# Sliding-window attention and a gated FFN on one core: key blocks of 64 on four TensorE tiles, and key blocks of 32 on eight

## The chip, the cores and the metric

The kernel runs on one core of a Trainium2 chip. The metric is the device time of one execution in microseconds, the median over runs. Each execution computes the whole output from inputs that lie in the chip's memory, weights included. TensorE does the matrix multiplications into PSUM (eight banks), ScalarE (ACT) and VectorE (DVE) take them out of it, GpSimd (POOL) and SyncE (SP) mostly issue transfers (DMA).

## The reference

Attention with 8 batches, 8 heads, 576 tokens, head size 64, in which a query sees itself and the 63 keys before it; its output, put together over the heads, goes through a gated feed-forward block.

```python
def _attn_ref(q, k, v):
    B, H, S, D = q.shape                       # 8, 8, 576, 64
    window = 64
    scores = (1.0 / np.sqrt(D)) * np.matmul(q, k.transpose(0, 1, 3, 2))
    rel = np.arange(S)[:, None] - np.arange(S)[None, :]
    scores = np.where((rel >= 0) & (rel < window), scores, -1000000000.0)
    scores = scores - np.max(scores, axis=-1, keepdims=True)
    attn = np.exp(scores)
    attn = attn / (np.sum(attn, axis=-1, keepdims=True) + 1e-09)
    return np.matmul(attn, v)

def _moe_ref(x, w_gate, w_val, w_out):         # x: 4608 x 512, weights 512 x 1536, 1536 x 512
    g = x @ w_gate
    return (g * (1.0 / (1.0 + np.exp(-g))) * (x @ w_val)) @ w_out
```

## The kernel before

The 4608 tokens are nine tiles of 512. Tile t = 0 to 6 is tokens 0 to 511 of batch t, tile 7 (`LAST`) the last 64 tokens of all eight batches, tile 8 tokens 0 to 511 of batch 7. Every operand of TensorE is bf16, sums are fp32 in PSUM. The order of instructions on each engine is written out by hand (`manual_schedule`): an engine runs its instructions in program order, and what one engine needs from another it waits for on semaphores.

One turn of the main loop (L740) is one tile t. First its attention, laced into the output projection of tile t - 1; then its gate and value products with the weights `wg` and `wv` (`gate_value`, L444): twelve blocks of 128 of the 1536 hidden columns, each eight matmuls of 512 columns (L448), a Silu on ACT (L441) and a multiplication on DVE into `hT` (L442). The projection of tile t (`project`, L488, matmuls L457) is four blocks s of 128 tokens, 12 matmuls of 512 columns each; `project_end` copies a block out of PSUM (L464) and stores it (L483).

Attention of a tile t from 1 to 6 and of tile 8, before the change. Queries and keys lie transposed: `queries[t]` and `kT` hold 64 features of an even head on partitions 0 to 63 (h = 0) and of an odd head on 64 to 127 (h = 1), for four pairs of heads u. Two pairs make a half w of the heads.

- `scores(t, w)` (L252): eight blocks j of 64 keys. A block meets the 128 queries from its own first key on, for two head pairs x and two heads h: four matmuls with 64 x 64 weights (L269), which lie in four quarters of the TensorE array. 32 matmuls for a half of the heads, 64 for a tile. ACT takes the exponential (L282) of two times 960 columns, DVE multiplies by a mask of ones and zeros (L285) and adds the two parts that a query's sum consists of into `both` (L290).
- `sums(t, w)` (L321): four matmuls of a matrix of ones with `both` (L302, 512 columns), then ACT takes the logarithm (L316) and the exponential of its negative (L319), which is the inverse of the sum.
- `mix_all(t)` (L416): 64 matmuls of the values with the exponentials (L386), then DVE multiplies by the inverse (`scale`, L402) into `xT`, the input of the gate.

TensorE's order in a tile is: scores of half 0; projection block 0 and five matmuls of block 1; scores of half 1 and sums of half 0; the rest of block 1 and block 2; sums of half 1 and the products; block 3; then the gates. In PSUM, `two[0]` and `two[1]` are two pairs of banks, for scores and products; `out_tile` gives banks 4 and 5 in turn to projection and gate, `d_tile` banks 6 and 7 to sums and values of the gate.

Loads: `load_qk(t + 2)` is issued on POOL's queue in the gates of tile t, q in four transfers (L91), k in sixteen (L126). DVE transposes one head pair at a time (`turn`: q at L207, k at L217) after gate blocks 1, 4, 7 and 10 of tile t - 1 (in tile 1's turn after blocks 6, 7, 9 and 10). v comes in eight transfers (`load_halves`, L152), on SP into a staging tile which POOL casts (L177), or on POOL directly. A run of 16 tokens of q is one row of a transfer, so queries are in the order of their place in a run: `blocks` (L68) picks the queries of some keys out of that order.

In tile 7 a query's two key blocks are not neighbours in one sequence, and `scores` and `mix` use twice as many matmuls, each with 64 queries.

Of the kernel before, what the change touches and what calls it, by code (L numbers as in the profile page):

```python
# [8 lines left out]
P = 128  # L9
# [8 lines left out]
def kernel(  # L18
# [13 lines left out]
    NT = NTOK // 512  # L32
    TURNED = 1
    LAST = NT - 2

    ctx.enter_context(tc.manual_schedule())
    cst = ctx.enter_context(tc.tile_pool(name="cst", bufs=1))
# [17 lines left out]
    vl = v12[:].rearrange("r g i (c w h) d -> r (g i) c w h d", c=2, w=2)  # L55
    vb = [cst.tile([P, 8, 2, 2, D], BF16, name=f"vb{i}") for i in range(2)]
    eb = [cst.tile([P, 17, 64], BF16, name=f"eb{i}") for i in range(4)]
    identb = cst.tile([P, P], BF16, name="identb")
    ones = cst.tile([P, 512], BF16, name="ones")
    tri = cst.tile([P, 2, 64], BF16, name="tri")  # L60
# [4 lines left out]
    def batch(t):  # L65
        return t if t < LAST else t - 1

# [80 lines left out]
    def load_halves(eng, dst, t, hds=range(H)):  # L148

        for hd in hds:  # L150
            w, x, h = hd // 4, hd // 2 % 2, hd % 2
            eng.dma_start(  # L152
                dst[64 * x:64 * x + 64, :, w, h],
                v[batch(t), hd, 0:512].rearrange("(j r) d -> r j d", r=64),
            )

    def load_last_v():
        for c in range(2):
# [11 lines left out]
    def stage_v(t):  # L170
        new_v(t)
        load_halves(nc.sync, staged[t, "v"], t)
# [30 lines left out]
    def turn_q(t, u):  # L203

        if u == 0:
            queries[t] = att.tile([P, 4, 512], BF16, name="qT", tag="qT")
        nc.vector.transpose(  # L207
            queries[t][:, u, :].rearrange("r (e x) -> r e x", e=16),
            staged[t][0][:, u].rearrange("r (e d) -> r e d", d=D)[:, :, 0:32],
        )  # L210
# [38 lines left out]
    def half(x):  # L249
        return slice(64 * x, 64 * x + 64)  # L250
# [57 lines left out]
    def room(n):  # L308
        return fsb.tile([P, 2, 512], FP32, name="r", tag="r", bufs=4)[:, 0:n]

    def turned(ap):

        return ap.rearrange("r (e x) -> r x e", e=16)

    def log(r, d_ps):
        nc.scalar.activation(r, d_ps, AF.Ln)  # L316
# [4 lines left out]
    def sums(t, w):  # L321
        d = d_tile(), d_tile()
        totals(t, w, d)
        for x in range(2):
            r = room(1)[:, 0]
            if t == NT - 1:
                log(r.rearrange("r (x e) -> r x e", e=16), turned(d[x]))
            else:
                log(r, d[x])
            invert(r)  # L330
            inverse[t, 2 * w + x] = r

# [62 lines left out]
    def scale(t, u, o_ps):  # L395
        if u == 0:
            xT[t] = att.tile([P, 4, 512], BF16, name="xT", tag="xT")
        x, r = xT[t][:, u, :], inverse.pop((t, u))
        if t == NT - 1:
            x, o_ps = x.rearrange("r (x e) -> r x e", e=16), turned(o_ps)  # L400
            r = r.rearrange("r (x e) -> r x e", e=16)
        nc.vector.tensor_mul(x, o_ps, r)  # L402

    taken = {"a": 0, "g": 0, "v": 0}
# [1 line left out]
    def take(tag):  # L406
        taken[tag] += 1
        return taken[tag] % 2 ^ 1
# [3 lines left out]

    def d_tile():
        return bank[6 + take("v")]

    def mix_all(t):  # L416
        tiles = wide(), wide()
# [26 lines left out]
    def gate_value(t, m):  # L444
        pair = gate_tiles()
        for ps, w in zip(pair, (wg, wv)):
            for c in range(4):
                nc.tensor.matmul(  # L448
                    ps[:], w[:, c, P * m:P * m + P], xT[t][:, c, :],
                    start=(c == 0), stop=(c == 3),  # L450
                )
        gate_end(t, m, pair)
# [9 lines left out]
    def project_end(t, s, o_ps, copy=nc.vector.tensor_copy):  # L462
        os_ = fsb.tile([P, 512], FP32, name="os_", tag="os_", bufs=4)
        copy(os_[:], o_ps[:])  # L464
        rows = out[S * batch(t):S * batch(t) + 512]
        if t < TURNED or t == NT - 1:
            if t < TURNED:
                rows = rows.rearrange("(r e) f -> e r f", e=4)[s]
            else:
                rows = rows[P * s:P * s + P]  # L470
            if t < TURNED or s == 0:
                for i in range(2):
                    nc.sync.dma_start(rows[half(i)], os_[half(i)])
            else:
                nc.sync.dma_start(rows, os_[:])
            return
# [197 lines left out]
    for m in range(12):  # L674
        if m < 4:
            if m == 2:
                pairs += [gate_tiles(), gate_tiles()]
                for i, w in enumerate((wg, wv)):
                    for n in (2, 3):
                        for c in range(4):  # L680
                            gate_one(0, n, pairs[n][i], w, c)
            gate_end(0, m, pairs[m])
        else:
            gate_value(0, m)
        if m == 3:
            for x in range(2):
                for c in range(2):
                    nc.vector.tensor_copy(
                        mask[half(x), 0, c],
                        tri[half(x), x ^ c].rearrange("r (y e) -> r e y", e=16),  # L690
                    )
            for i in (1, 2, 4):
                nc.vector.tensor_copy(mask[:, i:2 * i], mask[:, 0:i])
            for E in eb:
                nc.vector.memset(E[:, 0], 0.0)
        if m in (7, 10):
# [12 lines left out]
        if m == 9:  # L709
            for u in range(2):  # L710
                turn_q(1, u)
# [26 lines left out]
        project_end(0, s, tiles[s], on_a if s < 2 else on_v)  # L738

    for t in range(1, NT):  # L740
        if t > 1:
            set_exp()
            scores(t, 0)
            project(t - 1, 0)
            if t == 2:
                stage_v(3)
# [24 lines left out]
        turns = (6, 7, 9, 10) if t == 1 else (1, 4, 7, 10)  # L771
        for m in range(12):
            gate_value(t, m)
            if m in turns and t + 1 < NT:
# [35 lines left out]
```

## Time and profile before

| | us |
|---|---|
| runs, median of 3 (lowest, highest) | 324.4 (324.14, 324.52) |
| profiled execution, first to last instruction | 322.4 |
| TensorE busy in it | 317.1 |
| VectorE busy | 219.5 |
| ScalarE busy | 166.8 |
| GpSimd busy | 145.8 |
| attention stage of tile 2, from the last gate of tile 1 to the first of tile 2 (104.73 to 117.91) | 13.18 |

All times in views of the trace are microseconds from the span's start. A timeline line gives start, length, engine, source line, operation, the tile written and those read, the shape and how many instructions were put together; lengths of neighbouring groups overlap, since matmuls are pipelined: a matmul of 512 columns is recorded as 0.38 us long, and they start 0.22 us apart. A line of groups ends with the busy time, the mean length of one in ns, and after the next bar how long the engine had been idle before them and what ended most of that. "two", "one", "eb", "both" are the program's names of tiles; "issue" is time for which the profile shows no releaser.

### The profile page before, as it was taken

Reading aid. Unit: us, or ns where it says so; the run is one execution under the profiler, and the core shown is the slowest. Engines: PE = TensorE matmul, PEld = TensorE weight load, DVE = VectorE, ACT = ScalarE, POOL = GpSimd, SP = SyncE. Lnnn points to the kernel's source line nnn. Section 1 sums busy time; section 2 is a strip of 40 time slices with the busy share of each in tenths; the row PEclk is TensorE's granted clock in tenths of the full one; section 3 lists DMA queues with packets and bytes.
Section 4 is the critical chain, followed back from the end, with each engine's and each line's share of the span. In section 5 each row is a group of like instructions: output and inputs, shape, how many; then the busy total and the mean of one; then the engine's idle time right before and its main releaser. Section 6 shows DMA issues by size and latency. Waiting matters only on the chain.

```text
span 322.4 us, 7047 instructions
## 1 busy us (share of the span) xinstructions
PE 317.1 (98%) x2774; PEld 150.5 (47%) x2774; DVE 219.5 (68%) x349; ACT 166.8 (52%) x239; POOL 145.8 (45%) x259
## 2 busy tenths in 40 slices
PE   7999999999999999999999999999999999999995
PEld 3644444444544444444444544454444544444443
DVE  5866846597676867777688766876696586773432
ACT  5954665356633763368335833665347533773310
POOL 4955656966075795586125989462200000000000
PEclk9999999999999999999999999999999999999999
DMA  7999999999989999949903999799401400020012
GB/s 252 202 197 198 206 142 223 150 158 126 199 162 198 114 166 195 195 74 226 198 11 46 170 163 97 57 211 179 87 3 35 100 2 0 14 86 36 0 28 103
DMA packets 83521, 40.35 MB, mean 125 GB/s; under 512 B 64160, under 2 KB 78752, under 8 KB 83488
## 3 DMA queue, kind: packets, MB, share of 16 engines
q0 software_dynamic: 51488, 22.59, 58.3%
q1 hardware_dynamic: 31456, 16.79, 21.0%
q10 hardware_dynamic: 544, 0.52, 0.5%
q8 instruction: 21, 0.34, 0.4%
q14 instruction: 12, 0.10, 0.1%
HBM read 53.02 MB, written 9.44 MB: 194 GB/s over the span
## 4 chain that ended last, share of the span: by engine, by line
PE 95%; DMA 2%; DVE 1%; SPq 1%; issue 0%; DVEq 0%
PE one L448 56%; PE one L457 29%; PE two L269 3%; PE two L386 2%; DMA k_f<-in_k_dram 2%; PE one L424 2%; PE one L302 1%; PE one L499 1%; SPq L77 1%; PE two L424 1%; DVE kT L198 0%; PE two L702 0%; PE one L351 0%; DVE qT L573 0%; PE two L302 0%
## 5 line engine op out<-in xcount | busy, mean ns | idle before, releaser
L441 ACT ACTIVATE sg<-one 128x512 f32<-128x512 f32 x107 | 63.9, 597 | 113.6 <-PE one L448 86.7
L442 DVE TENSOR_TENSOR hT<-sg,one 128x512 bf16<-128x512 f32 x107 | 74.2, 694 | 61.9 <-PE one L448 57.8
L448 PE MATMUL one<-xT,wg 128*128 128x512 bf16 x416 | 106.8, 379 | 0.0
L448 PE MATMUL one<-xT,wv 128*128 128x512 bf16 x416 | 106.8, 379 | 0.0
L457 PE MATMUL one<-wo,hT 128*128 128x512 bf16 x420 | 95.2, 380 | 0.0
L126 POOL DMA_DIRECT2D k_s<-in_k_dram x112 | 60.8, 552 | 29.0 <-DMA q_s<-in_q_dram 21.8
L448 PEld LDWEIGHTS <-wv 128*128 128x128 bf16 x416 | 40.7, 98 | 49.1
L448 PEld LDWEIGHTS <-wg 128*128 128x128 bf16 x416 | 40.5, 98 | 48.8
L457 PEld LDWEIGHTS <-hT 128*128 128x128 bf16 x420 | 39.0, 98 | 46.7 <-issue 2.0
L282 ACT ACTIVATE eb<-two 128x960 bf16<-128x960 f32 (+1 forms) x32 | 29.5, 975 | 15.1 <-PE two L269 15.0
L217 DVE STREAM_TRANSPOSE kT<-k_s 128x512 bf16<-128x512 bf16 x28 | 36.1, 1289 | 0.0
L285 DVE TENSOR_TENSOR eb<-eb,mask 128x960 bf16<-128x960 bf16 (+1 forms) x32 | 21.1, 658 | 11.5 <-ACT eb L282 11.5
L402 DVE TENSOR_TENSOR xT<-two,r 128x512 bf16<-128x512 f32 x34 | 21.8, 686 | 6.4 <-PE two L386 4.8
L177 POOL CAST vb<-v_f 128x512 bf16<-128x512 f32 x20 | 11.5, 619 | 30.3 <-DMA v_f<-in_v_dram 19.4
L319 ACT ACTIVATE r<-r 128x512 f32<-128x512 f32 (+1 forms) x34 | 22.2, 657 | 1.0
L207 DVE STREAM_TRANSPOSE qT<-q_s 128x512 bf16<-128x512 bf16 x32 | 22.3, 701 | 0.1
L316 ACT ACTIVATE r<-one 128x512 f32<-128x512 f32 x31 | 18.3, 590 | 4.7 <-PE one L302 4.7
L91 POOL DMA_DIRECT2D q_s<-in_q_dram x24 | 13.1, 566 | 4.3 <-DVE qT L207 4.2
L290 DVE TENSOR_TENSOR both<-eb 128x512 bf16<-128x512 bf16 x32 | 13.6, 425 | 1.1
L152 POOL DMA_DIRECT2D vb<-in_v_dram x16 | 11.1, 718 | 4.6 <-DMA wo<-in_moe_w_out_dram 3.4
L507 ACT ACT_TABLE_LOAD x9 | 11.5, 1283 | 2.0 <-issue 1.9
L98 POOL DMA_DIRECT2D q_s<-in_q_dram x16 | 8.6, 627 | 7.5 <-DVE qT L207 7.5
(128 smaller groups left out, 198.4 us busy)
## 6 DMA issues: line engine op xcount, KB each, us to landing
k_s<-in_k_dram POOLq DMA_DIRECT2D x112, 56.0 KB, 4.8
q_s<-in_q_dram POOLq DMA_DIRECT2D x24, 248.0 KB, 5.9
v_f<-in_v_dram SPq DMA_DIRECT2D x40, 128.0 KB
wg<-in_moe_w_gate_dram POOLq DMA_DIRECT2D x5, 256.0 KB, 8.4
wv<-in_moe_w_val_dram POOLq DMA_DIRECT2D x5, 256.0 KB, 9.4
q_f<-in_q_dram SPq DMA_DIRECT2D x4, 256.0 KB
wo<-in_moe_w_out_dram POOLq DMA_DIRECT2D x2, 512.0 KB, 9.9
vb<-in_v_dram POOLq DMA_DIRECT2D x16, 64.0 KB, 4.6
```

Source lines behind the costliest of these rows:

```text
L126: nc.gpsimd.dma_start(k_s[p0:p0 + 32, g, :, 0:w], k[b, a:H:2, s:s + P].rearrange("u (r e) d -> r u (e d)", e=4) [:, :, 32 * c:32 * c + w],)
L207: nc.vector.transpose(queries[t][:, u, :].rearrange("r (e x) -> r e x", e=16), staged[t][0][:, u].rearrange("r (e d) -> r e d", d=D)[:, :, ...
L217: nc.vector.transpose(dst[:, u, :].rearrange("r (g x e) -> r g e x", g=4, e=4), k_s[:, :, u].rearrange("r g (e d) -> r g e d", d=D)[:, :, ...
L282: nc.scalar.activation(flat, s_ps[h][:].rearrange("r a b -> r (a b)")[:, 0:n], AF.Exp, scale=0.125)
L285: nc.vector.tensor_mul(flat, flat, mask[:].rearrange("r j c e y -> r (j c e y)")[:, 0:n])
L316: nc.scalar.activation(r, d_ps, AF.Ln)
L319: nc.scalar.activation(r, r, AF.Exp, scale=-1.0)
L402: nc.vector.tensor_mul(x, o_ps, r)
L441: nc.scalar.activation(sg[:], g_ps[:], AF.Silu)
L442: nc.vector.tensor_mul(hT[t][:, m, :], sg[:], v_ps[:])
L448: nc.tensor.matmul(ps[:], w[:, c, P * m:P * m + P], xT[t][:, c, :], start=(c == 0), stop=(c == 3),)
L457: nc.tensor.matmul(o_ps[:], hT[t][:, c, P * s:P * s + P], wo[:, c, :], start=(c == 0), stop=(c == 11),)
```

## The change

For six tiles (t = 2 to 6 and 8, `NARROW`) the attention is done in another form.

- Keys come in 16 blocks i of 32. A block meets the 96 queries from its first key on (64 and 32 at the end). A matmul has weights of 64 x 32 (`scores_n`) and, for the products and the sums, 32 x 64 (`mix_n`, `totals_n`): four head pairs u times two heads h lie on eight parts of the array. Scores are 128 matmuls, products 128, sums 8 of 512 columns.
- The four head pairs of a tile go together: scores in one visit, sums in one, products in one. The scores fill 960 columns of two bank pairs and 480 of banks 6 and 7; the exponential is taken in two pieces (960 and 480 columns) for each h. The mask multiplies only the first and the last third of each block's 96 queries. `both` is the sum of three parts.
- The logarithm and its exponential are taken over 1024 columns at a time. Products of u = 0 and 1 go to banks 6 and 7, of u = 2 and 3 to `two[0]`.
- TensorE's order becomes: seven matmuls of projection block 0; scores; the other five; block 1; three matmuls of block 2; sums; five of block 2; products; the last four; block 3. Block 0 is copied out by ACT.
- Queries come in runs of 8 tokens: q is loaded in eight transfers of half the row length, transposed with another output pattern, and the output is stored in two transfers of 64 rows for each block instead of four of 32. v is loaded to 32 partitions per head instead of 64.
- A mask for the new form is built once, in the gates of tile 1, in the place of `bias`, which only tile 0 uses.

```diff
+    NARROW = tuple(t for t in range(2, NT) if t != LAST)
...
+    en = [cst.tile([P, 49, 32], BF16, name=f"en{i}") for i in range(2)]
...
-            if t != LAST:
-                nc.gpsimd.dma_start(
-                    q_s[p0:p0 + 32, :, 0:w],
-                    q[batch(t), a:H:2, 0:512].rearrange("u (r e) d -> r u (e d)", e=16)
-                    [:, :, 32 * c:32 * c + w],
-                )
+            if t in NARROW:
+                for g in range(2):
+                    nc.gpsimd.dma_start(
+                        q_s[p0:p0 + 32, :, 512 * g:512 * g + 480],
+                        q[batch(t), a:H:2, 256 * g:256 * g + 256]
+                        .rearrange("u (r e) d -> r u (e d)", e=8)
+                        [:, :, 32 * c:32 * c + 480],
+                    )
...
+            if t in NARROW:
+                u = hd // 2
+                eng.dma_start(
+                    narrow_v(dst)[32 * u:32 * u + 32, :, h],
+                    v[batch(t), hd, 0:512].rearrange("(i r) d -> r i d", r=32),
+                )
+                continue
...
+    def scores_n(t):
+        qT = queries[t]
+        for i in range(16):
+            n = min(3, 16 - i)
+            b, o = (i // 5, 96 * (i % 5)) if i < 15 else (2, 448)
+            for u in range(4):
+                for h in range(2):
+                    s_ps = two[h][:, b] if b < 2 else bank[6 + h]
+                    nc.tensor.matmul(
+                        slots(s_ps[32 * u:32 * u + 32, o:o + 32 * n], n),
+                        kT[t % 2][half(h), u, 32 * i:32 * i + 32],
+                        block32(qT[half(h), u], i, n),
+                    )
+    def weigh_n(h):
+        flat = en[h][:, 4:49].rearrange("r b z -> r (b z)")
+        nc.scalar.activation(
+            flat[:, 0:960].rearrange("r (b z) -> r b z", b=2), two[h][:, :, 0:480],
+            AF.Exp, scale=0.125,
+        )
+        nc.scalar.activation(flat[:, 960:1440], bank[6 + h][:, 0:480], AF.Exp, scale=0.125)
+    def combine_n(t, h):
+        E = en[h]
+        slot = E[:, 4:49].rearrange("r (i s) z -> r i s z", s=3)
+        m = mask_n.rearrange("r i s e y -> r i s (e y)")
+        for i0, i1 in ((0, 10), (10, 15)):
+            nc.vector.tensor_mul(
+                slot[:, i0:i1, 0:3:2], slot[:, i0:i1, 0:3:2], m[:, i0:i1]
+            )
+        both = epool.tile([P, 16, 32], BF16, name="both", tag="both")
+        nc.vector.tensor_add(both[:], E[:, 2:48:3], E[:, 0:46:3])
+        nc.vector.tensor_add(both[:, 0:15], both[:, 0:15], E[:, 4:47:3])
+        nc.vector.tensor_add(both[:, 15], both[:, 15], E[:, 48])
+        weights[t, h] = both
+    def totals_n(t):
+        for u in range(4):
+            for h in range(2):
+                nc.tensor.matmul(
+                    two[u // 2][half(h), u % 2].rearrange("r (e n y) -> r n e y", e=8, n=16),
+                    ones[32 * u:32 * u + 32, 0:D],
+                    weights[t, h][32 * u:32 * u + 32].rearrange("r n (e y) -> r n e y", e=8),
+                )
+    def invert_n(t):
+        for w in range(2):
+            r = room(2)
...
+                log(r, two[w][:])
+            invert(r)
...
+    def out_n(u):
+        return bank[6 + u] if u < 2 else two[0][:, u - 2]
+    def mix_n(t):
+        vn = narrow_v(vb[t % 2])
+        for i in (*range(0, 16, 3), *range(1, 16, 3), *range(2, 16, 3)):
+            n, b = min(3, 16 - i), 4 + min(3 * i, 44)
+            for u in range(4):
+                r = slice(32 * u, 32 * u + 32)
+                for h in range(2):
+                    nc.tensor.matmul(
+                        block32(out_n(u)[half(h)], i, n), vn[r, i, h],
+                        en[h][r, b:b + n].rearrange("r n (e y) -> r n e y", e=8),
+                        start=i == 0, stop=i == 14,
+                    )
...
     for t in range(1, NT):
-        if t > 1:
+        if t in NARROW:
+            set_exp()
+            o_ps = out_tile()
+            project_part(t - 1, (0,), (o_ps,), range(7))
+            scores_n(t)
+            project_part(t - 1, (0,), (o_ps,), range(7, 12))
+            for h in range(2):
+                weigh_n(h)
+                combine_n(t, h)
+            project_end(t - 1, 0, o_ps, on_a)
+            if t == 2:
+                stage_v(3)
+            project(t - 1, 1)
+            o_ps = out_tile()
+            project_part(t - 1, (2,), (o_ps,), range(3))
+            totals_n(t)
+            invert_n(t)
+            project_part(t - 1, (2,), (o_ps,), range(3, 8))
+            mix_n(t)
+            project_part(t - 1, (2,), (o_ps,), range(8, 12))
+            for u in range(4):
+                if u == 2:
+                    project_end(t - 1, 2, o_ps)
+                scale(t, u, out_n(u))
+            project(t - 1, 3)
+        elif t > 1:
```

`block32` picks the queries of n blocks of 32 out of the order of runs of 8, `slots` views n of them side by side. Left out here are the new mask, the transposes' and the stores' patterns, and patterns of the last tile that follow the run length.

More of the change, by code (lines that the diff above doesn't have):

```diff
@@ L155, in load_halves, with narrow_v @@
             )
+    def narrow_v(dst):
+        return dst[:].rearrange("r j w h d -> r (j w) h d")
     def load_last_v():
@@ L206, in turn_q @@
             queries[t] = att.tile([P, 4, 512], BF16, name="qT", tag="qT")
+        if t in NARROW:
+            nc.vector.transpose(
+                queries[t][:, u, :].rearrange("r (e g x) -> r g e x", e=8, g=2),
+                staged[t][0][:, u].rearrange("r (g e d) -> r g e d", g=2, d=D)[:, :, :, 0:32],
+            )
+            return
         nc.vector.transpose(
@@ L311, in turned @@
     def turned(ap):
-        return ap.rearrange("r (e x) -> r x e", e=16)
+        return ap.rearrange("r (e x) -> r x e", e=8)
     def log(r, d_ps):
@@ L325, in sums @@
             r = room(1)[:, 0]
[L326 to L329, printed above, removed]
+            log(r, d[x])
             invert(r)
@@ L399, in scale @@
         if t == NT - 1:
-            x, o_ps = x.rearrange("r (x e) -> r x e", e=16), turned(o_ps)
-            r = r.rearrange("r (x e) -> r x e", e=16)
+            x, o_ps = x.rearrange("r (x e) -> r x e", e=8), turned(o_ps)
+            r = r.rearrange("r (x e) -> r x e", e=8)
         nc.vector.tensor_mul(x, o_ps, r)
@@ L414, in d_tile, with block32, slots @@
         return bank[6 + take("v")]
+    mask_n = bias[:].rearrange("r a e i c x -> r (a e i c x)")[:, 0:960].rearrange(
+        "r (i s e y) -> r i s e y", i=15, s=2, e=8
+    )
+    def block32(ap, i, n):
+        return ap.rearrange("r (e x) -> r e x", e=8)[:, :, 4 * i:4 * i + 4 * n].rearrange(
+            "r e (n y) -> r n e y", n=n
+        )
+    def slots(ap, n):
+        return ap.rearrange("r (n e y) -> r n e y", n=n, e=8)
+    def scores_n(t):
[11 more added lines that the diff above has]
+                    )
@@ new lines, in weigh_n @@
+    def weigh_n(h):
[12 more added lines that the diff above has]
+                slot[:, i0:i1, 0:3:2], slot[:, i0:i1, 0:3:2], m[:, i0:i1]
+            )
+        both = epool.tile([P, 16, 32], BF16, name="both", tag="both")
[3 more added lines that the diff above has]
+        weights[t, h] = both
@@ new lines, in totals_n @@
+    def totals_n(t):
[5 more added lines that the diff above has]
+                    weights[t, h][32 * u:32 * u + 32].rearrange("r n (e y) -> r n e y", e=8),
+                )
+    def invert_n(t):
+        for w in range(2):
+            r = room(2)
+            if t == NT - 1:
+                log(
+                    r.rearrange("r b (x e) -> r b x e", e=8),
+                    two[w][:].rearrange("r b (e x) -> r b x e", e=8),
+                )
+            else:
+                log(r, two[w][:])
+            invert(r)
+            for x in range(2):
+                inverse[t, 2 * w + x] = r[:, x]
@@ new lines, in out_n @@
+    def out_n(u):
[11 more added lines that the diff above has]
+                        start=i == 0, stop=i == 14,
+                    )
@@ L475, in project_end @@
                 nc.sync.dma_start(rows, os_[:])
+            return
+        if t in NARROW:
+            rows = rows.rearrange("(x e) f -> e x f", e=8)
+            for i in range(2):
+                nc.sync.dma_start(rows[2 * s + i], os_[half(i)])
             return
@@ L695 @@
                 nc.vector.memset(E[:, 0], 0.0)
+            for E in en:
+                nc.vector.memset(E[:, 0:4], 0.0)
         if m in (7, 10):
@@ L740 @@
     for t in range(1, NT):
-        if t > 1:
+        if t in NARROW:
+            set_exp()
[23 more added lines that the diff above has]
+        elif t > 1:
             set_exp()
@@ L744 @@
             project(t - 1, 0)
-            if t == 2:
-                stage_v(3)
             o_ps = out_tile()
@@ L773 @@
             gate_value(t, m)
+            if t == 1 and m == 3:
+                for u in range(4):
+                    for s in range(2):
+                        r, z = slice(32 * u, 32 * u + 32), 32 * (u % 2)
+                        nc.vector.tensor_copy(
+                            mask_n[r, 0, s],
+                            tri[r, (u // 2) ^ s, z:z + 32].rearrange("r (y e) -> r e y", e=8),
+                        )
+                for i in (1, 2, 4):
+                    nc.vector.tensor_copy(mask_n[:, i:2 * i], mask_n[:, 0:i])
+                nc.vector.tensor_copy(mask_n[:, 8:15], mask_n[:, 0:7])
+                nc.vector.tensor_copy(mask_n[:, 14, 1], mask_n[:, 0, 0])
             if m in turns and t + 1 < NT:
```

## The prediction

> **What bounds the kernel now.** I read the busy times and the clock row first, then the chain of waits, then the timeline of one attention stage (tile 2, TensorE alone) and of the last tile's, then the groups by line.
>
> ```profile
> PE 317.1 (98%) x2774; PEld 150.5 (47%) x2774; DVE 219.5 (68%) x349; ACT 166.8 (52%) x239; POOL 145.8 (45%) x259
> ...
> PEclk9999999999999999999999999999999999999999
> ...
> PE 95%; DMA 2%; DVE 1%; SPq 1%; issue 0%; DVEq 0%
> ```
>
> TensorE is busy 98% of the span at full clock, and 95% of the chain that ends last is TensorE. So a change is worth what it adds to or takes from TensorE's stream, waits in that stream included. DVE and ACT count only where TensorE waits for them.
>
> The timeline of TensorE from 103.6 us (start, length, line, operation, count):
>
> ```profile
> 103.87 1.03 PE L448 MATMUL one<-xT,wv 128*128 128x512 bf16 x4
> 104.82 0.62 PE L269 MATMUL two<-qT,kT 64*64 64x128 bf16 x32
> 105.37 3.84 PE L457 MATMUL one<-wo,hT 128*128 128x512 bf16 x17
> 109.15 0.62 PE L269 MATMUL two<-qT,kT 64*64 64x128 bf16 x32
> 109.60 0.39 PE L302 MATMUL one<-both,ones 64*64 64x512 bf16 x4
> 109.92 4.27 PE L457 MATMUL one<-wo,hT 128*128 128x512 bf16 x19
> 114.12 0.41 PE L302 MATMUL one<-both,ones 64*64 64x512 bf16 x4
> 114.36 1.01 PE L386 MATMUL two<-eb,vb 64*64 64x128 bf16 x64
> 115.31 2.76 PE L457 MATMUL one<-wo,hT 128*128 128x512 bf16 x12
> 117.91 0.38 PE L448 MATMUL one<-xT,wg 128*128 128x512 bf16 x1
> ```
>
> A full-size matmul steps by 0.2165 us (12 of L457 in 117.91 - 115.31 = 2.60). The last gate group ends its step at 103.87 + 4 x 0.2165 = 104.73; the next gate starts at 117.91. Of these 13.18 us, 48 full-size matmuls take 10.39, so attention costs TensorE 2.79 us in three visits: 104.73 to 105.37 = 0.64 (scores of half the heads); 109.05 to 109.92 = 0.87 (the other scores, half the sums; 109.05 is 105.37 + 17 x 0.2165); 114.03 to 115.31 = 1.28 (the other sums, the products). Tiles 3 and 8 take the same 13.18 us.
>
> **What an issued matmul costs.** The last tile (t = 7) already uses pieces of 64 queries, so twice the matmuls of half the length:
>
> ```profile
> 240.41 0.71 PE L269 MATMUL two<-qT,kT 64*64 64x64 bf16 x64
> ...
> 250.13 1.35 PE L386 MATMUL two<-eb,v 64*64 64x64 bf16 x128
> 251.41 0.82 PE L457 MATMUL one<-wo,hT 128*128 128x512 bf16 x3
> ```
>
> A group's length less one matmul (0.19 us) is the time from first to last start. 64 matmuls of 128 columns: 0.82/63 = 13.0 ns each. 64 of 64 columns: 0.52/63 = 8.3 ns; 128 of them: 1.16/127 = 9.1 ns, and the 64 of these that the window from 250.6 to 251.0 us touches are 0.74 long, 8.7 ns each. Half the columns do not halve the step (13.0 to 8.3-9.1): something per matmul with its weight load is becoming the limit.
>
> **Matmuls of the change.** Per tile, scores and products go from 64 matmuls each to 128, of 96 columns instead of 128, on eight array tiles instead of four. No row shows eight at once. From below: waves of eight at the step of a wave of four. A wave of four is 4 x 13.0 = 52 ns at 128 columns and 4 x 8.3 = 33 at 64, so about 43 at 96; 16 waves are 0.69 us. From above: no more than four at once, 32 waves x 43 = 1.38 us. Between them: the matmuls come at 8.3 to 9.1 ns whatever the array does, 127 x 8.4 = 1.07 us. I take this: it is the nearest row, with the same count of instructions, and a wave of eight at 43 ns would need 5.4 ns per matmul, which no burst here reaches.
>
> By the Trainium skill (TensorE: Matmul & The Clock Gate, "Measured speedup vs the span model") a further array tile costs about 4 ns of issue, sixteen tiles at once gained 10.6 times, so eight would fit in a wave. By it the sum would be that of the lower end. The last tile's rows do not bear it out in a long burst: 4 tiles, 9.1 ns each.
>
> Visits after, per tile. Entry 104.82 - 104.73 = 0.09; exit from the last start (115.18) to 115.31 = 0.13. Scores: 0.09 + 1.07 + 0.13 = 1.29. Sums: 8 matmuls of 512 columns, all eight array tiles, instead of two groups of four: 0.09 + 0.32 (109.60 to 109.92) = 0.41; the other group with its entry goes. If only four ran at once: 0.21 more. Products: 1.29 and the wait below. Together 2.99 against 2.79: +0.20.
>
> **Waits in the stream**, counted from the last gate's end (104.73 is 0):
> - Scores now need all four head pairs. Seven matmuls lead: 1.52 + 0.09 = 1.61. The last pair's transposes (L207, L217) end at 106.17, that is 1.44; L442 of the last gate, which frees banks 6 and 7, at 106.68, 1.95, and the first matmul on them is the 81st, at 1.61 + 0.67 = 2.28. No wait, 0.17 to spare.
> - Sums need both exps, masks and adds:
>
> ```profile
> L282 ACT ACTIVATE eb<-two 128x960 bf16<-128x960 f32 x28 | 25.7, 968 | 13.0 <-PE two L269 12.9
> ...
> L316 ACT ACTIVATE r<-two 128x1024 f32<-128x1024 f32 x2 | 1.9, 1020 | 2.1 <-PE two L302 2.1
> ```
> ```profile
> L285 DVE TENSOR_TENSOR eb<-eb,mask 128x960 bf16<-128x960 bf16 x28 | 18.3, 654 | 9.6 <-ACT eb L282 9.6
> L290 DVE TENSOR_TENSOR both<-eb 128x512 bf16<-128x512 bf16 x32 | 13.6, 425 | 1.1
> ```
>
> (Groups with shapes apart: busy us, mean ns.) DVE: 512 elements 425 ns, 960 take 654, so 0.51 ns an element and 0.16 fixed. Per half: masks of 640 and 320 (0.49 + 0.33), adds of 512, 480 and 32 (0.43 + 0.41 + 0.18) = 1.84, less some 0.17 of overlap of independent neighbours. ACT starts 0.23 after the 80th matmul (L269 to L282 at 109.81), at 2.51; its first 960 end at 3.48; DVE ends at 3.52 + 2 x 1.67 + 0.15 = 7.0. TensorE comes there at 1.61 + 1.07 + 0.13 + 20 x 0.2165 + 0.09 = 7.23. No wait, 0.2 to spare. Price if the strided masks ran at one element a cycle (twice 0.51 ns, 0.98 us more for both halves): 0.75 us a tile.
> - Products for half the heads go to the banks that log reads: sums start + 0.50 (114.12 to 114.62) + 1.02 + 0.05 = 1.57; TensorE is there after 0.32 + 5 x 0.2165 + 0.09 = 1.49: +0.09 with the restart.
> - The gate needs four scales and a copy: 5 x 0.68 + 0.2 = 3.6 us after the products; TensorE has 16 matmuls, 3.47, and uses the fourth scale 0.65 later. Covered.
>
> **Parts at nothing.** DVE loses 4 x 0.654 + 4 x 0.425 - 2 x 1.84 = 0.6 us a tile and a copy (L464) that ACT takes; neither is on the chain. Not quite nothing: the new mask takes DVE some 3 us once, in tile 1's gate (eight copies of 32 elements at 0.2, five of 32 to 448 at 0.2 to 0.45, by L688's 272 ns for 64 and L693's 510 for 512). DVE idles 1.04 of every 1.73 us there (before L442), so the next L442 is 2.0 late; its bank is written again 1.6 us after L442 ends (88.33 - 86.70 in tile 2's gate): 0.3 us, once. q comes in eight DMAs of half the rows' length instead of four: 4 x 0.545 = 2.2 us more on POOL (L91), ahead of k, L152's v and the cast. For tile 2, the tightest, POOL idles 4.1 us between 46.6 and 58.3, waiting for q's landings, and the last k issue (58.32) lands by about 63.1; the transpose takes it at 63.70. Without that cover: 2 us, once. v comes in as many DMAs, to 32 partitions each; out goes in two instead of four per block (L483, SP), which has idle time.
>
> So +0.20 + 0.09 = +0.29 us a tile, x 6 = +1.7, with the mask's 0.3: +2.0 us on a span of 322.4. The runs' median is 324.4: 2.0 lie around the span and stay. Forecast 326.4; its own range 325.1 to 328.0.
>
> **Rivals.**
> - Faster: waves of eight at 43 ns. Both bursts 0.69 instead of 1.07, -0.76 a tile; the waits shrink less, since ACT and DVE take what they took: sums 0.1, log 0.09. 2.79 becomes 0.91 + 0.51 + 1.00 = 2.42, -0.37 to -0.47 (the latter if the sums do not wait), x 6, and the mask: 321.9 to 322.5. It decides below 7.3 ns a start (0.29 us less over 254 starts). It is the span model's case. For it: 8.3 ns at four tiles of 64 may still be the array's limit (33 ns for 64 columns). Against: 128 in a row fell to 9.1.
> - Slower by the wait for `both`: masks with 32-element runs at one element a cycle. +0.75 a tile from the moment the DVE chain is over 0.2 us longer: 326.4 + 4.5 = 330.9. Every DVE row here has longer runs. By the Trainium skill (VectorE: DVE Perf Modes, "What auto-detection actually checks") 16-bit tensors of step 1 keep two elements a cycle, which would leave this at nothing.
> - Slower by four at once: bursts 1.38, sums 0.21 longer: +0.83, x 6: 331.4. In the scores each partition feeds four array tiles, where it feeds two now; no row excludes a limit there.
> - It does nothing: matmuls that queue during the full-size ones before a visit start closer together, bursts about 0.95, waits gone: -0.04 a tile, and the mask: 324.5.
>
> **Chances.** Forecast 0.40, faster 0.25, no change 0.15, masks 0.10, four at once 0.10. A run of this kernel tells 0.2% (0.65 us) from no change. Faster by more than that: the rival and a little of "no change", 0.28. Within: 0.14. Slower: 0.58. Cases of both signs hold much, so the range goes a little past the faster rival and takes in the slower ones: 321.5 to 331.4.
>
> **What would show it.** In the profile after: scores and products as groups of 128 at 8 to 9 ns a start (forecast), 5.4 (rival), or 10.8 (four at once); the sums as one group of 8, 0.32 us to the next full-size matmul; no TensorE idle named for DVE `both`; masks of 640 elements at 0.49 us, not 0.8; attention's share of a stage 3.1 us. The forecast is wrong if the bursts step below 7.3 ns or if TensorE stands at the sums.

## The result and the profile after

The changed kernel takes 330.2 us (median of 4 runs, 328.38 to 330.67), the kernel before beside it 324.5 (324.14 to 325.21): a ratio of 1.016, 95% interval 1.013 to 1.019, so 5.8 us slower. The forecast was 2.0 us slower. In three of the four runs the mean granted clock is 0.995 and in the fourth, 328.38 us, it is 1.000; the half clock shown below, 1.7 us, fits that gap. The profiled execution spans 328.5 us, 6.1 more than before.

The page of the changed kernel (busy times, clock row, chain by engine, and the queue that brings instructions):

```profile
PE 317.8 (97%) x3505; PEld 153.8 (47%) x3542; DVE 211.1 (64%) x370; ACT 160.9 (49%) x221; POOL 158.1 (48%) x283
...
PEclk9999999999999999999999899999999999999999
...
q8 instruction: 27, 0.44, 0.6%
...
PE 95%; issue 2%; DMA 1%; ACT 1%; DVE 0%; DVEq 0%
```

TensorE's busy time has grown by 0.7 us only. New are a dent in the clock row (the 8) and 2% of the chain under "issue", time in which TensorE stood and waited for nothing in the program. The instruction queue carried 27 packets of 16 KB. Its line before the change:

```profile
q8 instruction: 21, 0.34, 0.4%
```

A stage as the forecast meant it, tile 3, TensorE alone (start, length, line, tiles, shape, count). The stage that the text ahead of this section calls tile 2's, 104.73 to 117.91, lies between the gates of tile 2 and of tile 3, so it is tile 3's, the same as this one:

```profile
107.59 0.85 PE L455 MATMUL two<-qT,kT 64*32 64x96 bf16 x80
108.23 0.60 PE L455 MATMUL one<-qT,kT 64*32 64x96 bf16 x48
109.00 4.26 PE L565 MATMUL one<-wo,hT 128*128 128x512 bf16 x19 [0.16 <-issue]
113.19 0.42 PE L488 MATMUL two<-both,ones 32*64 32x512 bf16 x8
113.55 1.25 PE L565 MATMUL one<-wo,hT 128*128 128x512 bf16 x5
```

The 128 score matmuls start within 1.06 us, 8.3 ns each; the sums go as one group of eight with 0.36 us to the next full-size matmul. (The bracket behind 109.00 is the missing record of one L565, not a wait.) From the last gate matmul to the next gate's first, this stage takes 13.606 us against 13.392 before, counted start to start: +0.214. Tiles 4 and 6 give +0.21 too. Tile 5 gives +3.91. This is its products' end:

```profile
183.99 0.23 PE L518 MATMUL one<-en,vb 32*64 32x64 bf16 x4
184.02 0.21 PE L518 MATMUL two<-en,vb 32*64 32x64 bf16 x1
186.05 0.22 PE L518 MATMUL two<-en,vb 32*64 32x64 bf16 x3 [1.82 <-issue]
186.42 4.87 PE L565 MATMUL one<-wo,hT 128*128 128x512 bf16 x14 [0.16 <-issue]
```

Three matmuls from the end of the burst TensorE stands for 2.02 us between two starts, with no releaser. The windows of the same time (us; busy PE, PEld, DVE, ACT, POOL with counts; granted clock, DMA share, GB/s):

```profile
181.00:184.00 3.00, 3.00 (x138) 1.57 (x136) 0.77 (x3) 2.04 (x3) 3.00 (x7) 1.00 1.04 193
184.00:186.00 2.00, 0.23 (x30) 0.13 (x16) 1.29 (x2) 1.97 (x3) 1.18 (x3) 1.00 1.07 218
186.00:187.00 1.00, 0.80 (x6) 0.43 (x7) 0.00 (x0) 0.98 (x2) 0.99 (x2) 0.86 1.16 159
187.00:190.00 3.00, 3.00 (x9) 1.08 (x8) 1.89 (x3) 0.34 (x1) 3.00 (x7) 0.50 1.06 118
190.00:193.00 3.00, 3.00 (x15) 1.40 (x14) 0.69 (x1) 0.59 (x1) 3.00 (x6) 0.98 1.09 173
```

After the stop the granted clock is half for 3.41 us (186.72 to 190.13 in the clock record). Full-size matmuls step by 0.427 us in it, which costs 1.7 us more. In the kernel before TensorE is busy through the whole of 184 to 186:

```profile
184.00:186.00 2.00, 2.00 (x11) 0.94 (x10) 1.55 (x4) 1.95 (x3) 2.00 (x5) 1.00 1.14 219
```

The 6.1 us of the span: stop and half clock 3.70; six tiles by 0.214, 1.28; the mask in tile 1's gate 0.13; smaller delays in tiles 2, 4, 7 and 8, 0.51; and 0.78 at the start, where the full clock came at 5.8 us instead of 4.3; 0.3 less at the end.

### The profile page after: what moved, and what is told of

It reads as the page before. It is cut to its first block, busy times and chain, and to the rows that moved or that the text cites. A ratio compares the mean times of both kernels' runs of the same rounds, so it can differ in the third digit from the quotient of the medians.

```text
span 328.5 us, 8519 instructions
## 1 busy us (share of the span) xinstructions
PE 317.8 (97%) x3505; PEld 153.8 (47%) x3542; DVE 211.1 (64%) x370; ACT 160.9 (49%) x221; POOL 158.1 (48%) x283
## 4 chain that ended last, share of the span: by engine, by line
PE 95%; issue 2%; DMA 1%; ACT 1%; DVE 0%; DVEq 0%
PE one L556 54%; PE one L565 28%; PE one L532 2%; PE two L455 1%; PE one L518 1%; DMA q_f<-in_q_dram 1%; PE two L518 1%; PE one L612 1%; PE two L289 1%; PE one L455 1%; PE two L403 1%; PE two L488 1%; PE two L532 1%; PE one L209 0%; ACT qk_b L677 0%
## 5 line engine op out<-in xcount | busy, mean ns | idle before, releaser
L556 PE MATMUL one<-xT,wv 128*128 128x512 bf16 x408 | 106.2, 379 | 0.5
L556 PE MATMUL one<-xT,wg 128*128 128x512 bf16 x406 | 105.9, 379 | 0.5
L565 PE MATMUL one<-wo,hT 128*128 128x512 bf16 x402 | 94.4, 384 | 2.4 <-issue 2.2
L556 PEld LDWEIGHTS <-wv 128*128 128x128 bf16 x416 | 40.7, 98 | 49.3 <-issue 0.4
L556 PEld LDWEIGHTS <-wg 128*128 128x128 bf16 x416 | 40.5, 98 | 48.8
L565 PEld LDWEIGHTS <-hT 128*128 128x128 bf16 x420 | 39.5, 99 | 47.6 <-issue 4.2
L94 POOL DMA_DIRECT2D q_s<-in_q_dram x48 | 25.8, 546 | 8.5 <-DVE qT L222 7.9
L336 ACT ACTIVATE r<-two 128x1024 f32<-128x1024 f32 (+1 forms) x15 | 14.7, 988 | 13.6 <-PE two L488 11.5
L339 ACT ACTIVATE r<-r 128x1024 f32<-128x1024 f32 (+1 forms) x22 | 19.7, 902 | 0.6
L419 DVE TENSOR_TENSOR xT<-one,r 128x512 bf16<-128x512 f32 x14 | 9.0, 687 | 16.2 <-PE two L518 10.6
L419 DVE TENSOR_TENSOR xT<-two,r 128x512 bf16<-128x512 f32 x22 | 14.0, 683 | 4.9 <-PE two L403 4.4
L222 DVE STREAM_TRANSPOSE qT<-q_s 128x512 bf16<-128x512 bf16 x24 | 16.8, 701 | 0.0
L476 DVE TENSOR_TENSOR en<-en,bias 128x640 bf16<-128x640 bf16 (+1 forms) x24 | 9.0, 405 | 11.1 <-ACT en L464 11.1
L464 ACT ACTIVATE en<-two 128x960 bf16<-128x960 f32 x12 | 11.7, 974 | 7.8 <-PE two L455 7.8
L176 POOL DMA_DIRECT2D v<-in_v_dram x16 | 10.9, 732 | 1.0 <-issue 1.0
```

The lines of the kernel that those rows point to most:

```text
L94: nc.gpsimd.dma_start(q_s[p0:p0 + 32, :, 512 * g:512 * g + 480], q[batch(t), a:H:2, 256 * g:256 * g + 256] .rearrange("u (r e) d -> r u (e ...
L222: nc.vector.transpose(queries[t][:, u, :].rearrange("r (e g x) -> r g e x", e=8, g=2), staged[t][0][:, u].rearrange("r (g e d) -> r g e d" ...
L339: nc.scalar.activation(r, r, AF.Exp, scale=-1.0)
L464: nc.scalar.activation(flat[:, 0:960].rearrange("r (b z) -> r b z", b=2), two[h][:, :, 0:480], AF.Exp, scale=0.125,)
L556: nc.tensor.matmul(ps[:], w[:, c, P * m:P * m + P], xT[t][:, c, :], start=(c == 0), stop=(c == 3),)
L565: nc.tensor.matmul(o_ps[:], hT[t][:, c, P * s:P * s + P], wo[:, c, :], start=(c == 0), stop=(c == 11),)
```

## Experiments

The rows of TensorE's instruction list, each matmul two (weights and product), can be counted in the trace by its weight loads: the stop lies at row 4288, a few rows short of the burst's end. 27 packets for 7084 rows are about 262 rows each. **Theory:** instructions arrive in blocks of 256 rows, and a burst of 256 rows in 1.07 us uses one up before the next is there; 4288 is then a block end, the end before it lies 5 rows ahead of the burst, and the place depends on the row count alone. **Rivals:** something in tile 5 itself (data, transfers, the time of the run); the TensorE array; the visits.

**e1: 96 rows further on.** 60 small warm-ups take the place of 12.

```diff
-    for _ in range(6):
-        nc.tensor.matmul(warm[0:D, 0:P], ones[:, 0:D], ones[:, 0:P])
-    keep_warm(6)
+    for _ in range(60):
+        nc.tensor.matmul(warm[0:D, 0:64], ones[:, 0:D], ones[:, 0:64])
```

> The changed kernel, but its 12 warm-up matmuls at the start are cut into 60 shorter ones (the same 3840 columns): 48 more matmuls, each with its weight load, put 96 rows of TensorE's instruction list ahead of everything else; the work is the same. Theory (instruction supply): TensorE's list comes in packets of about 256 rows, and tile 5's products stood still for 2.0 us because their 256 rows began 5 rows behind the end of a packet, so that the next packet was needed 1 us after the last; with 96 rows more that burst begins 101 rows behind an end, and the 2 us stop leaves tile 5. Tile 3's products then begin 5 rows behind an end and may stop for up to 2 us. Time 326 to 330.2 us, by whether tile 3 stops. Rival (something of tile 5 itself, such as its transfers, a semaphore or the clock): the stop stays in tile 5's products, 2.0 us, and the time stays at 330.2.

330.1 us (329.19 to 330.86, 5 runs). Windows of e1 around tile 3's products, and tile 5's:

```profile
115.00:118.00 3.00, 0.86 (x96) 0.76 (x88) 1.29 (x2) 2.95 (x4) 2.96 (x6) 0.93 1.00 140
118.00:121.00 3.00, 2.67 (x9) 1.11 (x10) 0.93 (x2) 0.93 (x1) 2.69 (x5) 0.50 1.09 120
...
184.00:186.00 2.00, 2.00 (x17) 0.73 (x15) 1.31 (x4) 0.50 (x1) 1.41 (x3) 1.00 0.93 156
```

The stop (2.3 us) and its half clock are now in tile 3, whose products start 5 rows behind a block end in this kernel; tile 5 has none. So it is a matter of rows, not of tile 5.

**e2: 24 rows further on**, 18 warm-ups of 170 columns for the last six.

```diff
-    keep_warm(6)
+    for _ in range(18):
+        nc.tensor.matmul(warm[0:D, 0:170], ones[:, 0:D], ones[:, 0:170])
```

> As e1_shift96, with 24 rows more instead of 96 (24 warm-up matmuls for 12). By the theory of the instruction supply no burst of products of any tile begins between 14 rows before and 26 rows behind the end of a packet: no stop above 0.3 us anywhere, clock at full speed throughout, six attention stages of 13.6 us each, 324.46 + 6 x 0.21 + 0.13 = 325.9 us and up to 0.8 us for the start, 325.9 to 326.7. Rival (tile 5 itself): the 2.0 us stop and the halved clock stay, 330.2 us.

328.1 us (326.83 to 329.02, 6 runs): no long stop, but not the time expected. Tile 5's products still stand 0.43 us (they start 29 rows behind an end). Another 1.04 us go at 151.57, between full-size matmuls just behind tile 4's products; there one end lies 19 rows after the burst's start and the next 19 rows after its last row. The danger reaches further on both sides than I had put it.

**e3: scores twice**, each matmul issued two times in a row, the second writing the same values.

```diff
-        for i in range(16):
+        for i in [i for i in range(16) for _ in range(2)]:
```

> The changed kernel with each score matmul issued twice in a row by blocks, the second over the first: 512 rows of instructions in one burst. If TensorE's own step of 8.3 ns is all that matters, each burst takes 2.13 instead of 1.06 us, + 6 x 1.07 = 6.4 us: 336.6. By the theory of the instruction supply every burst must cross the ends of two packets within 2 us, and most of the six stop for 0.5 to 2 us besides, some with the clock halved after: 339 to 350 us.

355.5 us (one run). 512 rows at 8.3 ns a pair would be 2.1 us; five of the six bursts took 4.5 to 5.3. The sixth, tile 6's, took 2.13, and TensorE stopped behind it. The first burst, and TensorE's waits of e3 (us in total, times, longest):

```profile
73.00:76.00 3.00, 3.00 (x214) 2.15 (x213) 1.77 (x3) 0.94 (x2) 3.00 (x6) 1.00 1.14 118
76.00:79.00 3.00, 0.66 (x70) 0.56 (x60) 0.49 (x1) 0.81 (x2) 2.22 (x5) 1.00 1.07 114
```
```profile
PE one L455 <- issue: 10.6, 4, 2.9
PE one L565 <- issue: 4.5, 15, 2.0
PE two L455 <- issue: 2.5, 1, 2.5
```

The scores, which never stood still in the changed kernel, stand for 13.1 us in five places once a burst has two blocks' worth of rows. That is more than the 339 to 350 expected, and it is the supply.

**e4: 128 columns** in the scores instead of 96; the last 32 of each are written over by the next block.

```diff
-            n = min(3, 16 - i)
+            n = min(4, 16 - i)
```

> The changed kernel with 128 instead of 96 queries in each score matmul; the 32 surplus columns are overwritten by the next block's. Theory: matmuls come at 8.3 ns because that is the step of issue, not because eight tiles of 96 columns fill the array: bursts stay at 1.06 us from first to last start, time within 0.5 us of the changed kernel. Rival (the array is the limit, 67 ns for a wave of eight with 96 columns): a third more columns make 1.4 us, + 6 x 0.35 = 2.1 us.

330.05 us (one run). Score bursts of 1.14 to 1.16 us in tiles 3 to 6 instead of 1.06: a third more columns for 8% more time. So something that hardly grows with the columns sets the step; I call it issue. The stop is at the same place (2.4 us).

**e5 and e8: 176 rows further on**, 100 warm-ups of 38 columns (e5) and of 64 (e8).

```diff
-    for _ in range(6):
-        nc.tensor.matmul(warm[0:D, 0:P], ones[:, 0:D], ones[:, 0:P])
-    keep_warm(6)
+    for _ in range(100):
+        nc.tensor.matmul(warm[0:D, 0:38], ones[:, 0:D], ones[:, 0:38])
```

> 100 warm-up matmuls of 38 columns take the place of the twelve at the start (as much TensorE time), so every later instruction lies 176 rows further on. Theory (instructions come in blocks of 256 rows, and a burst in which a second block end falls too soon after the first starves): the products start 37 (tile 2), 85, 133, 181, 229 (tile 6) and 69 (tile 8) rows behind a block end; stops were seen at 5 and 29 behind an end and 19 rows after a burst that started at 237. So no stop of 2 us and no half clock anywhere; tile 5's products last 1.07 us; at most one stop of 0.5 to 1 us, in tile 2's products (37) or just behind tile 6's (229). Time 326.0 to 327.2 us. Rival (the stop is an affair of tile 5, of its data or its transfers, and e1 and e2 moved it by chance): 2 us again in some tile's products and half clock behind it, 329 to 330.5. Rival (the longer program itself costs): above 330.2.

> The 176 rows of shift again, with 100 warm-ups of 64 columns instead of 38. With 38 the full clock began at 11.0 us instead of 5.8 and the first gate at 30.97 instead of 29.02. Theory (the shift removed the stop in tile 5 and its half clock, and e5's start hid 1.9 us of that): start as in the changed kernel, every later stage as in e5, the 1.2 us stop behind tile 6's products with it: 327.2 to 327.8 us. Rival (the first blocks of instructions come late because the warm-up is longer, whatever its columns): the first gate stays at 30.9, 329.3.

e5: 329.3 us (328.84 to 329.5, 4 runs); e8: 328.5 (327.88 to 328.69, 4 runs). In both, tile 5's products last 1.04 us, the clock stays full, and one of the two places named beforehand is hit: behind tile 6's products. In e5 TensorE loses 1.20 us there between two starts, more than the 0.5 to 1 expected:

```profile
220.03 2.98 PE L565 MATMUL one<-wo,hT 128*128 128x512 bf16 x13
224.05 0.81 PE L565 MATMUL one<-wo,hT 128*128 128x512 bf16 x3 [1.04 <-issue]
```

The times were off: e5's start was 1.9 us late (the full clock came at 11.0 us). With e8's wider warm-ups a point in tile 0's gate that the changed kernel passes at 29.02 and e5 at 30.97 comes at 29.72, and tile 2's products (37 rows behind an end) stand 0.52 us, which they had not in e5. In e8 the instruction packet before them took 1.97 us (79.26 to 81.23), in e5 1.16 (80.53 to 81.69). So e8's expected 327.2 to 327.8 was missed by what these two take. Neither shift frees all tiles: successive tiles' products lie 48 rows apart against the blocks, so with six tiles some burst is always close to a block end.

**e6: products in two halves** with two projection matmuls between them.

```diff
-            mix_n(t)
-            project_part(t - 1, (2,), (o_ps,), range(8, 12))
+            mix_n(t, slice(0, 8))
+            project_part(t - 1, (2,), (o_ps,), range(8, 10))
+            mix_n(t, slice(8, 16))
+            project_part(t - 1, (2,), (o_ps,), range(10, 12))
```

> The products are issued in two bursts of 64 matmuls with two matmuls of the projection (L565) between them; no matmul more or less, and no row number moves but those of these two. Theory (instruction supply): 0.65 us more for the same 256 rows, so the stop in tile 5's products (2.02 us) shrinks to at most 0.7 us and the half clock behind it (1.7 us) goes; the second visit costs 0.09 + 0.13 = 0.22 us in each of six tiles. 330.2 - 3.0 to 3.7 + 1.3 = 327.8 to 328.5. Rival (the stop belongs to that row of the program whatever comes before it): it stays, with its half clock, and the visits are added: 331.5. Forecast's sum if there was no stop to begin with and the visits are all: 331.5 as well.

329.3 us (328.28 to 331.07, 5 runs); the profiled one is the 331.07. It and the 330.37 have a mean granted clock of 0.995, the other three 1.000. In the profiled one the expected gain did not come: in tile 5's second half

```profile
185.17 0.23 PE L518 MATMUL one<-en,vb 32*64 32x64 bf16 x3
186.98 0.18 PE L518 MATMUL one<-en,vb 32*64 32x64 bf16 x1 [1.58 <-issue]
```

it stands 1.79 us instead of 2.02, and the half clock follows. The 0.65 us that I gave it are small against what a block needs: in the five traces with this stop, TensorE goes on 3.0 to 3.5 us after the burst's first start.

**e7: four array tiles in succession** instead of eight, in the scores.

```diff
-        for i in range(16):
+        for i, us in [(i, us) for us in ((0, 1), (2, 3)) for i in range(16)]:
...
-            for u in range(4):
+            for u in us:
```

> The scores' 128 matmuls go through the key blocks twice, first for two head pairs and then for the other two, so that only four array tiles follow each other instead of eight; count, columns and rows stay. If the array sets the step at four tiles (96 columns on four tiles, 43 ns a wave by the forecast): 10 to 10.8 ns a start, bursts of 1.27 to 1.37 us instead of 1.06, and 331.5 us in all. If only the issue of a matmul with its weight load sets it: 8.3 ns, 1.06 us, 330.2. The stop in tile 5's products stays in both.

330.08 us (one run); score bursts of 1.30 us in tiles 3 to 5, 10.2 ns a start. Tile 3 of e7:

```profile
107.25 0.64 PE L455 MATMUL two<-qT,kT 64*32 64x96 bf16 x40
...
108.30 0.42 PE L455 MATMUL one<-qT,kT 64*32 64x96 bf16 x24
108.65 1.69 PE L565 MATMUL one<-wo,hT 128*128 128x512 bf16 x7
```

With four tiles the step is the one expected if the array sets it; eight tiles gain on four, down to the 8.3 ns of issue. The stop (2.04 us) is in tile 5's products again, but no half clock follows. The expected 331.5 had its 1.7 us in it.

**e9: tile 5 as before the change**, all other tiles as after it. Tile 5 then has exactly 256 rows less, so every later tile keeps its place against the blocks.

```diff
-    NARROW = tuple(t for t in range(2, NT) if t != LAST)
+    NARROW = tuple(t for t in range(2, NT) if t not in (5, LAST))
```

(With it, tile 5's q is loaded by the four transfers of the kernel before.)

> Tile 5 alone is done as in the kernel before (key blocks of 64, bursts of 32 and 64, runs of 16 tokens), the other five as changed. Its bursts are half as long, so no two block ends fall into one; tile 5 has exactly 256 rows less, so every later tile keeps its place against the blocks. Theory (supply): 330.2 - 3.7 (stop and half clock) - 0.2 (visits) = 326.3, with 0.4 to either side for the start; no stop over 0.3 us. Forecast's own sum for five tiles without any supply term, at the measured 0.21 a tile and 0.13 for the mask: 325.7 plus what the start takes. Rival (the stop comes at that time of the run or that part of the program, whatever burst is there): 329 to 330.

326.4 us (325.9 to 327.5, 6 runs), a ratio to before of 1.006, 1.004 to 1.008. TensorE's waits and clock row in e9:

```profile
PEclk9999999999999999999999999999999999999999
```
```profile
PE one L571 <- issue: 1.9, 12, 0.2
PE one L562 <- issue: 0.2, 1, 0.2
```

(L571 is L565 of the changed kernel; these 12 are missing records of the kind at 109.00 above. L562 is the gates' L556; the 0.2 counts from the recorded end of a matmul, but two starts, 154.09 and 154.69, lie 0.60 apart, 0.38 more than a step. That is a little over the 0.3 allowed for.) No stop of 0.4 us or more is left and the time falls by 3.8, of which 0.2 is tile 5's visits. One tile in six held two thirds of the loss.

**The block's arrival.** In the records of the instruction queue, each packet is 16,384 bytes. Where TensorE stood, it went on a nearly fixed time after one packet's end:

| kernel, place | packet from + length | TensorE goes on | after the packet's end |
|---|---|---|---|
| after, tile 5 | 183.71 + 0.96 | 186.05 | 1.38 |
| e1, tile 3 | 115.15 + 1.43 | 117.95 | 1.37 |
| e2, behind tile 4 | 150.55 + 0.95 | 152.82 | 1.32 |
| e4, tile 5 | 183.68 + 0.97 | 186.08 | 1.43 |
| e5, behind tile 6 | 221.61 + 0.99 | 224.05 | 1.45 |
| e6, tile 5 | 184.44 + 1.01 | 186.98 | 1.53 |
| e7, tile 5 | 184.56 + 0.97 | 186.92 | 1.39 |
| e8, behind tile 6 | 220.81 + 0.98 | 223.12 | 1.33 |

Seven stops of e3 give 1.20 to 1.56. Stops of 1.0 to 3.1 us in five parts of the program all end by the same rule, which no affair of one tile would do.

They also begin by one rule. All fifteen lie at a row that is 192 more than a multiple of 256: 4288 in the changed kernel, e4, e6 and e7, 2752 in e1, 3520 in e2, 5312 in e5 and e8. In each of the eleven traces the queue carries exactly as many packets as the list has such rows: 21 before, 27 after, 33 in e3. So a block is 256 rows, and the place of a stop goes by the row count.

## Why the prediction was right or wrong

The sign was right, and so was what the forecast said of the visits: +0.20 a tile, measured +0.21. But six tiles make 1.28 of 5.8 us. The size, 2.0, was wrong because 3.7 us come from something that the working does not have. That 330.2 lies inside the stated 321.5 to 331.4 is luck: the upper end stood there for the slow masks and for four at once, and neither came.

- **Where the sum failed:** in the part "Waits in the stream", at the products. It listed the log wait (+0.09) as their only wait and took the burst's 8.4 ns a start as holding for any burst. That TensorE can run out of instructions was not a term. e1, e5, e8 and e9 show that it is: 2.0 us of stop and, in most runs, 1.7 of half clock. The page of before had the hint, 21 packets of 16 KB on the instruction queue, and the working doubled the rows of a burst without asking how fast rows come. The row that I took for long bursts, the last tile's 128 products, misled me: as many rows, and no stop in any trace here. In the kernel before, the block ends around it lie 5.70 us apart (245.10, and 250.80 inside the burst) and the packet sets out at 245.93, so the next block had time to come.
- **Burst, 8.4 ns a start, 1.07 us:** measured 8.3 and 1.06 (scores), 1.07 (products).
- **Visits 2.99 a tile:** measured 1.268 + 0.447 + 1.279 = 2.99 (tile 3 of e5, where no record is missing).
- **Scores, no wait, 0.17 to spare:** read in tile 3's stage, it holds there and in the later tiles. In tile 2 the keys of the last head pair are transposed later, up to 1.73 us after the last gate instead of 1.44 (it ends at 72.57 before, 73.47 after). The seventh score matmul, the first of that pair, starts at 73.52, and tile 2's stage is 0.13 longer than tile 3's.
- **Log wait 0.09:** it is not there; the product visit begins 0.09 us behind the last full-size matmul, like every other. Per tile +0.214 came out instead of +0.29, for six tiles 1.28 instead of 1.7.
- **Mask, 0.3 once:** 0.13 in this trace (tile 1's gate 20.632 against 20.504). In e1, e2 and e4 to e9, which build the same mask, that gate takes 20.50 as before, so mostly it costs nothing.
- **No wait at the sums:** right. The DVE groups of the changed kernel (busy, mean ns):

```profile
L476 DVE TENSOR_TENSOR en<-en,bias 128x640 bf16<-128x640 bf16 x12 | 5.9, 488 | 11.1 <-ACT en L464 11.1
L480 DVE TENSOR_TENSOR both<-en 128x512 bf16<-128x512 bf16 x12 | 5.1, 425 | 0.4
L481 DVE TENSOR_TENSOR both<-both,en 128x480 bf16<-128x480 bf16 x12 | 4.9, 408 | 0.4
L476 DVE TENSOR_TENSOR en<-en,bias 128x320 bf16<-128x320 bf16 x12 | 3.9, 322 | 0.0
L482 DVE TENSOR_TENSOR both<-both,en 128x32 bf16<-128x32 bf16 x12 | 2.0, 168 | 0.0
```

  The mask of 640 takes 488 ns where 0.49 us was put down, so the rival of masks at one element a cycle falls.
- **Rival, waves of eight at 43 ns:** falls. 8.3 ns a start, not 5.4, and e4 shows that columns hardly count. The Trainium skill (TensorE: Matmul & The Clock Gate, "Measured speedup vs the span model") has some 4 ns for each further array tile; here, with a weight load for every matmul, it is twice that.
- **Rival, four at once, 331.4:** its time came close (330.2) by another way. e7 shows what four in succession cost, 1.30 us a burst; the changed kernel has 1.06. It falls.
- **Loads and POOL at nothing:** no TensorE wait names a transfer in the changed kernel.
- **Start:** 0.78 us of the profiled span. Kernels with the same warm-ups pass the point that the changed kernel passes at 29.02 between 28.50 (e7) and 29.79 (e3), where before passed it at 28.24. One trace of before doesn't tell whether the change has a part in it.

The scores escape where their packet sets out early. In e5's tile 8 they begin 3 rows behind a block end, pass two ends 1.58 us apart (281.05 and 282.63) and do not stop: the packet had set out at 278.44, during the gates, 2.6 us before the first of the two. For tile 5's products in the changed kernel it set out 1.45 us after the first. That TensorE's sequencer reads ahead during the long gates would fit, and was not tested.

Not settled: 0.14 in tile 7 and 0.19 in tile 8 beyond the visits; why a packet sets out 0.7 us behind its burst's first start in one place and 2.8 in another, with which the danger zone widens; and what sets a packet's length, 0.88 to 1.97 us in these traces, which no experiment varied. A version that beats the kernel before is not in sight: even without any stop, six tiles lose 0.21 each.

## What to carry to other kernels

Doubling the instructions of a burst is a cost in itself, even when each runs as fast as forecast: count the rows of TensorE's list (a matmul with its weights is two) and ask how long 256 of them last. Where TensorE stopped for a microsecond or more here, 3.0 to 5.2 us lay between the block end before and the first use of the next block. Two block ends with a dense burst between them could stop it for up to 2.4 us, and for 3.1 in a burst of 512 rows. A wait named "issue" at one place of a repeated loop, and nowhere else, points to this; moving the program by some rows moves the stop, and that tells it from something in the place itself.

## What the runs showed of the hardware

- **Instruction supply.** Packets of 16,384 bytes, 256 rows each; TensorE, where it stood, goes on 1.20 to 1.56 us after the packet's end. The Trainium skill (Runtime: NRT & Kernel Launch, "Instruction fetch mechanics") has the blocks of 256 instructions, and says the fetch is mostly hidden since instructions are issued more slowly than they arrive. The blocks agree with the row counts here; the second part does not hold for bursts of small matmuls at 8.3 ns a pair, where TensorE stood for 1.0 to 3.1 us.
- **Issue.** A matmul with its weight load starts every 8.3 ns on eight array tiles at 96 columns and about 9.0 at 128 (e4); on four array tiles at 96 columns every 10.2 (e7).
- **Clock.** A stop of 1.8 to 2.4 us was followed by a half clock of 3.41 us in four kernels (after, e1, e4, e6) and by none in e7 (2.0); in e3 three of six stops of 2.1 to 3.1 us were. All seven half clocks set in at a whole multiple of 3.413 us after the full clock had last begun: 180.91 us in the changed kernel, 53 times, and 112.64 in e1, 33 times. So a fixed grid of time seems to place it, not the stop's end. What decides whether it comes is open.
